# A fixed instruction order per engine in a pre-norm attention and GEGLU block, and another heir for two PSUM banks

## The chip, the core and the metric

One NeuronCore of a Trainium2 chip runs the whole program. Its engines are TensorE (PE in the profile; PEld is its loading of weights), VectorE (DVE), ScalarE (ACT), GpSimd (POOL) and SyncE (SP), which here issues nearly all DMAs. Each works through its own list of instructions in order, and waits on semaphores for the others. The metric is device microseconds per execution; several executions give a median.

## The reference, cut to what matters

x is 2048 rows of 512 floats. There are 32 heads of width 16 and four segments of 512 rows; attention is causal and inside a segment, and a running memory M, z joins the segments.

```python
h = x + A(layernorm(x))            # A: attention, then @ wo
out = h + B(layernorm(h))          # B: (gelu(y @ w_gate) * (y @ w_up)) @ w_down
# A, for segment s, heads in parallel:
p = softmax(qs @ ks.T / 4 + mask);  a_dot = p @ vs
a_mem = (phi(qs) @ M) / (phi(qs) @ z + 1e-6)       # phi(t) = t+1 if t>0 else exp(t)
o = g * a_mem + (1 - g) * a_dot                    # g = sigmoid(beta)
M += phi(ks).T @ vs;  z += sum(phi(ks))
```

The hidden width of B is 1376.

## The kernel before, in words

**Numbers.** Products are made in a reduced float type (fp32r) from operands split in two: a rounded copy on ScalarE (the "high" half) and the rest by a subtraction on VectorE or GpSimd. Three matmuls (SPLIT) make one product. So one entry of TensorE's order is often three 512-column matmuls.

**Attention.** Sixteen units U (four groups of eight heads, four segments) are cut into 32 halves Q of four heads each. For a unit, qkv projects (L634, the first time L646 for two at once) and moves the results by DMA into tiles stq and stk; vproj makes the values (L675); transposes (L754) and a small product (L762) renew the memory; mem reads it (L792 and L808 on TensorE, L810 on VectorE). For a half, two passes over the scores follow:

- pass_a, the row-maximum pass: scores into a bank of pool PA (L835), a masked maximum on VectorE (L843), small steps (L859, L862), a transpose (L866), and a DMA that puts the negated maximum as one more row into stq.
- pass_b, the other score pass: transposed scores, shifted by that row, into a bank of pool PB (L914, for the last diagonal block L906), the exponential on ScalarE (L922), masking on GpSimd (L925), and the product with the values in 32-column matmuls side by side in TensorE's four column groups (L946), into a bank of pool PPV. A half has eleven such score groups.

In the very last half, fill() in pass_b (L895) repeats a score matmul into a bank that pool PX holds at that time, up to ten times; nothing reads it.

**Seam and feed-forward.** wo_seg multiplies by wo per segment (operand split L1012 and L1014, matmuls L1019, sum L1023); ln2 normalises (L523, L575) and transposes (L594). The feed-forward runs twice over 1024 rows, in eleven hidden blocks f of 128 (the last 96); each block is seven products (prod, L1191; a Strassen-like scheme on two-by-two blocks), the gate (L1198 to L1222) and, for one or two blocks at a time, down (L1256, added up by L1264 and stored by L1269). Its weights are loaded into raw tiles (L1154), split (L1159 on ScalarE, L1161 on GpSimd) and combined (L1168 on GpSimd).

**PSUM.** Eight banks: three in PD, two in PA, two in PB, one in PPV. When nothing waits for a pool any more, its banks go to the pool named in `then`: PA's to PX, PB's and PPV's to PYZ (X, Y, Z are the banks of the feed-forward's products).

**What sets the order.** The code first registers 5308 groups of instructions with S.op, each with an engine, an assumed duration, a priority (formed from unit numbers and the table DUE) and the tiles that it reads, writes or takes. Nothing is issued by that. The group registered n-th has number n. Then Sched.run makes the order of all engines by list scheduling: among groups whose predecessors are placed and for which a buffer is free, it takes the earliest possible ones and among these the one with the lowest priority. It keeps a clock for each engine from the assumed durations; the clock also decides which of several free buffers a group gets. Where TensorE changes between normal matmuls (mode "f") and those in column groups (mode "c"), the clock adds DRAIN.

Each group is issued on its engine when it is placed, so the order in which run() places the groups of one engine is that engine's program.

## Time and profile before

| | us |
|---|---|
| median of 3 runs (823.0 to 824.62) | 824.03 |
| span of the profiled execution, first to last instruction | 820.5 |
| TensorE busy in it | 805.0 |
| VectorE busy | 615.2 |
| ScalarE busy | 561.7 |
| GpSimd busy | 483.8 |

The median is 3.5 us above the span, which begins with the first instruction and ends with the last. Busy time is the time in which at least one instruction of the engine runs; idle time in a row stands in brackets with the engine, tile and line that ended it. In tables of waits a row gives who waited, for whom, the sum in us, how often, and the longest. A weight load that waits stands for its matmul, which follows it in the same queue.

### The profile page before, as it was taken

Reading aid. Unit: us, or ns where it says so; the run is one execution under the profiler, and the core shown is the slowest. Engines: PE = TensorE matmul, PEld = TensorE weight load, DVE = VectorE, ACT = ScalarE, POOL = GpSimd, SP = SyncE. Lnnn points to the kernel's source line nnn. Section 1 sums busy time; section 2 is a strip of 40 time slices with the busy share of each in tenths; the row PEclk is TensorE's granted clock in tenths of the full one; section 3 lists DMA queues with packets and bytes.
Section 4 is the critical chain, followed back from the end, with each engine's and each line's share of the span. In section 5 each row is a group of like instructions: output and inputs, shape, how many; then the busy total and the mean of one; then the engine's idle time right before and its main releaser. Section 6 shows DMA issues by size and latency. Waiting matters only on the chain.

```text
span 820.5 us, 15349 instructions
## 1 busy us (share of the span) xinstructions
PE 805.0 (98%) x4728; PEld 629.1 (77%) x4728; DVE 615.2 (75%) x1823; ACT 561.7 (68%) x1131; POOL 483.8 (59%) x720
## 2 busy tenths in 40 slices
PE   7999999999999999999999999999999999999998
PEld 5786878777786877767666687878888887888886
DVE  7998778798898877799878764666657867565666
ACT  8689677899877868777676753786566454646450
POOL 8334334455344644456566884987797676869660
PEclk9999999999999999999999999999999999999999
DMA  7544445465564654466465763531211341212102
GB/s 243 143 115 131 133 126 135 131 199 157 139 176 115 185 157 122 124 172 186 140 188 165 234 205 125 165 93 52 65 39 52 108 152 38 78 40 64 52 1 102
DMA packets 71893, 103.51 MB, mean 126 GB/s; under 512 B 14340, under 2 KB 25156, under 8 KB 71812
## 3 DMA queue, kind: packets, MB, share of 16 engines
q1 hardware_dynamic: 71476, 102.15, 42.8%
q8 instruction: 37, 0.61, 0.3%
q10 hardware_dynamic: 336, 0.39, 0.2%
q14 instruction: 44, 0.36, 0.1%
HBM read 54.92 MB, written 21.43 MB: 93 GB/s over the span
## 4 chain that ended last, share of the span: by engine, by line
PE 88%; POOL 4%; DVE 4%; ACT 2%; issue 1%; DMA 1%; SPq 0%; POOLq 0%; ACTq 0%; DVEq 0%
PE bank L1191 23%; PE bank L1256 14%; PE bank L634 10%; PE bank L835 9%; PE bank L946 8%; PE bank L914 8%; PE bank L675 5%; PE bank L1019 5%; PE bank L762 1%; PE bank L808 1%; PE bank L594 1%; DVE bank L843 1%; PE bank L906 1%; POOL raw L1168 1%; DVE row L575 1%
## 5 line engine op out<-in xcount | busy, mean ns | idle before, releaser
L925 POOL TENSOR_SCALAR_AFFINE_SELECT pt<-pt 128x128 f32<-128x128 f32 (+2 forms) x352 | 119.4, 347 | 186.7 <-ACT pt L922 179.8
L922 ACT ACTIVATE pt<-bank 128x512 f32<-128x512 f32 (+1 forms) x352 | 182.2, 558 | 41.7 <-PE bank L914 32.2
L843 DVE CUSTOM_DVE_ANT_0 bank<-bank,amask 128x512 f32<-128x512 f32 (+1 forms) x256 | 157.0, 638 | 22.5 <-PE bank L835 20.7
L835 PE MATMUL bank<-stk,stq 128*128 128x512 f32 (+2 forms) x384 | 127.0, 374 | 0.6 <-DVE nm L843 0.2
L914 PE MATMUL bank<-stq,stk 128*128 128x384 f32 (+2 forms) x384 | 117.2, 359 | 2.1 <-ACT pt L922 2.0
L634 PE MATMUL bank<-xt,w 128*128 128x512 f32 x360 | 102.5, 396 | 0.1
L1264 DVE TENSOR_TENSOR pt<-pt,bank 128x512 f32<-128x512 f32 x95 | 64.4, 686 | 34.1 <-PE bank L1256 33.9
L843 DVE CUSTOM_DVE_ANT_0 aside<-bank,amask 128x256 f32<-128x256 f32 (+1 forms) x256 | 76.3, 353 | 14.2 <-PE bank L835 13.0
L914 PEld LDWEIGHTS bank<-stq,stk 128*128 128x128 f32 x384 | 68.0, 189 | 22.0 <-ACT pt L922 7.8
L835 PEld LDWEIGHTS bank<-stk,stq 128*128 128x128 f32 x384 | 68.7, 188 | 18.8 <-DVE nm L843 4.5
L946 PE MATMUL bank<-pt,vaug 128*32 128x512 f32 (+3 forms) x1024 | 76.9, 436 | 0.0
L634 PEld LDWEIGHTS bank<-xt,w 128*128 128x128 f32 x360 | 65.1, 188 | 10.5 <-DVE xt L604 0.4
L946 PEld LDWEIGHTS bank<-pt,vaug 128*32 128x32 f32 x1024 | 28.8, 109 | 40.2 <-issue 32.4
L843 DVE DVE_READ_ACCUMULATOR2_ANT nm<- 128x1 f32 x512 | 57.0, 111 | 0.0
L675 PE MATMUL bank<-wv,xt 128*128 128x256 f32 x384 | 55.6, 283 | 1.1 <-POOL wv L459 1.1
L675 PEld LDWEIGHTS bank<-wv,xt 128*128 128x128 f32 x384 | 52.4, 189 | 3.4 <-POOL wv L459 1.3
L443 POOL TENSOR_TENSOR w<-raw,w 128x512 fp32r<-128x512 f32 (+1 forms) x28 | 36.1, 1296 | 26.1 <-ACT w L438 25.9
L1161 POOL TENSOR_TENSOR w<-raw,w 128x512 fp32r<-128x512 f32 (+3 forms) x30 | 35.1, 1170 | 15.8 <-ACT w L1159 7.8
L1191 PE MATMUL bank<-xt,w 128*128 128x512 f32 (+1 forms) x159 | 43.5, 390 | 0.0
L1191 PE MATMUL bank<-xt,stk 128*128 128x512 f32 (+1 forms) x138 | 38.3, 391 | 0.0
L1161 POOL TENSOR_TENSOR stk<-raw,stk 128x512 fp32r<-128x512 f32 (+3 forms) x27 | 30.0, 1114 | 12.4 <-ACT stk L1159 12.3
L967 ACT ACTIVATE pvs<-bank 128x512 f32<-128x512 f32 x32 | 19.2, 599 | 26.1 <-PE bank L946 15.1
(305 smaller groups left out, 1873.6 us busy)
## 6 DMA issues: line engine op xcount, KB each, us to landing
stq<-hl SPq DMA_DIRECT2D x96, 128.0 KB
stk<-hl SPq DMA_DIRECT2D x188, 64.0 KB
pv_dram<-pvs SPq DMA_DIRECT2D x32, 256.0 KB
r<-r_dram SPq DMA_DIRECT2D x28, 256.0 KB
row<-x SPq DMA_DIRECT2D x24, 256.0 KB
raw<-wg SPq DMA_DIRECT2D x20, 256.0 KB
raw<-wu SPq DMA_DIRECT2D x20, 256.0 KB
raw<-wd SPq DMA_DIRECT2D x20, 256.0 KB
```

What stands on the lines that cost most here:

```text
L634: nc.tensor.matmul(pm.t, w.t[:, wi, dc * P:(dc + 1) * P], XT[s][dc].t[:, xi, :], start=dc == 0 and n == 0, stop=dc == ND - 1 and n == 2)
L675: nc.tensor.matmul(pm.t[:, 256 * t:256 * t + 256], XT[s][dc].t[:, xi, t0:t0 + P], whl[wi].t[:, h, 256 * (dc % 2):256 * (dc % 2) + 256], st ...
L835: nc.tensor.matmul(sa.t[:, k * w:(k + n) * w].rearrange("x (n w) -> x n w", n=n), sq.t[:, p, i * P:(i + 1) * P], sk.t[:, p, a:a + n, 0:w], ...
L843: nc.vector.tensor_tensor_reduce(out=(sa.t if i > 1 else aside)[:, k * w:(k + 1) * w], in0=sa.t[:, k * w:(k + 1) * w], in1=amask[:, D - w: ...
L914: nc.tensor.matmul(sc.t[:, lo:lo + D - q0], sk.t[:, p, a, q0:q0 + P], sq.t[:, p, q0:D], start=True, stop=True)
L922: act(w, prio, lambda: nc.scalar.activation(e.t[:, :w], sc.t[:, :w], AF.Exp), [sc], [e])
L925: nc.gpsimd.affine_select(v, v, pattern=pat + [[1, P]], compare_op=OP.is_ge, fill=0.0, base=0, channel_multiplier=-1)
L946: nc.tensor.matmul(pv.t[32 * n:32 * n + 32, kb * P:D], va.t[:, 136 * kb + 17 * j:136 * kb + 17 * j + 32], e.t[:, lo:lo + D - kb * P], star ...
L1161: pool(0.14 + 2.13e-3 * (hi - lo), prio, lambda: nc.gpsimd.tensor_tensor(v.t[:, 1, :hi - lo], r.t[:, lo:hi], v.t[:, 0, :hi - lo].bitcast(F ...
L1191: nc.tensor.matmul(dst.t[:w], v.t[:, wi, c0 + j * w:c0 + (j + 1) * w], b[bk][j].t[:, xi, :], start=first and j == 0 and n == 0, stop=j == ...
L1256: nc.tensor.matmul(pm.t[:, cs], HH[p, f, s][hi].t[:w, t * P:(t + 1) * P], v.t[:w, wi, cs], start=f == fl[0] and n == 0, stop=f == fl[-1] a ...
L1264: dve(W_, prio, lambda a=a, pm=pm, cs=cs, to=to: nc.vector.tensor_tensor(to.t[:, cs], a.t[:, cs], pm.t[:, cs], op=OP.add), [pm, a], [to])
```

## The change

It has four parts.

1. A list ORDER of 5308 numbers is added, and run() places the groups in this order, whatever their priority. The clock stays, for the choice of buffers; window, stay and DUE have no influence any more.
2. PA's two banks go to PB once nothing waits for PA, and PB's four go, once nothing waits for PB, one each to PX, PYZ, PX, PYZ. Before, PA's went straight to PX and PB's to PYZ.
3. The assumed durations of some TensorE groups (project, both score passes) rise by 0.004 to 0.012 us.
4. The code of the groups themselves is as before; every group of before is in the list once.

Groups that the text below speaks of by number: 43, 46 and 49 load the first wq, wk and wv (L437, L454); 930 to 932 load rows of the third segment (L614); 3303 and 3304 are the last memory product (L808) and its VectorE step (L810); 3494 is the last score group of the last half; 3593 and 3661 are the first transposes (L594) of the two norms at the seam, 3659 one of the last VectorE steps (L575) ahead of the latter; 3820 is the weights' rest (L443) of the third hidden block's down projection; 3857 and 3858 are the first split (L1159, L1161) of the fourth hidden block's weights and 4014 the first product (L1191) with them; 3758, 3759, 3768 and 3769 are operand splits of wo_seg (L1012, L1014).

```diff
+ORDER = [
+    6, 7, 5, 8, 2, 0, 4, 59, 13, 1, 3, 10, 930, 931, 932, 11, 9, 58, 30, 56, 57, 43, 46, 49, 12, 14, 15, 16, 17,
...
+    3476, 3477, 3660, 3482, 3483, 3303, 3479, 3480, 3382, 3658, 3487, 3491, 3659, 3494, 3485, 3486, 3821, 3304,
+    3488, 3489, 3661, 3667, 3535, 3536, 3700, 3492, 3493, 3824, 3495, 3496, 3458, 3662, 3663, 3713, 3701, 3668,
...
+    3745, 3756, 3750, 3957, 3715, 3958, 3751, 3960, 3857, 3820, 3856, 3752, 4626, 3962, 3858, 3757, 4627, 3753,
+    3758, 3766, 3963, 3964, 3754, 3961, 4014, 3859, 3759, 4017, 4015, 3860, 3767, 4016, 3869, 3760, 3755, 3965,
...
+]
...
-    def run(self, window=0.059, stay=0.1):
+    def run(self, order):
...
-        cand = [o for o in self.ops if o.n == 0]
-        order = []
+        done = []
...
-            first = min(e[0] for e in best)
-            _, at, o = min((e for e in best if e[0] <= first + window),
-                           key=lambda e: (e[2].prio, e[2].idx))
-            cand.remove(o)
...
+        for i in order:
+            o = self.ops[i]
+            assert o.n == 0, "an instruction comes before what it needs"
...
-    PA = Pool_(banks[3:5], then=PX)
-    PB = Pool_(banks[5:7], then=PYZ)
+    PB = Pool_(banks[5:7], then=Parts(1, PX, PYZ, PX, PYZ))
+    PA = Pool_(banks[3:5], then=PB)
...
-            pe(3 * mm(D), prio, f, [w, XT[s][dc]], [pm], acq=acq)
+            pe(3 * mm(D) + 0.012, prio, f, [w, XT[s][dc]], [pm], acq=acq)
...
-            m = mm(2 * w if i < 2 else w)
+            m = mm(2 * w if i < 2 else w) + 0.006
...
-                pe(2 * mm(2 * P), prio, f, [k3, q3], [sc], acq=[e], tail=mm(2 * P))
+                pe(2 * mm(2 * P) + 0.004, prio, f, [k3, q3], [sc], acq=[e], tail=mm(2 * P))
             else:
-                pe(len(parts) * mm(D - kb * P), prio, f, [sq, sk, mr], [sc], acq=[e],
+                pe(len(parts) * (mm(D - kb * P) + 0.005), prio, f, [sq, sk, mr], [sc], acq=[e],
                    tail=mm(D - kb * P))
...
-    return S.run()
+    return S.run(ORDER)
```

## The prediction

> **What bounds the kernel now.** I read the page first: how busy each engine is, then TensorE's and GpSimd's lines of the 40 slices.

> ```profile
> span 820.5 us, 15349 instructions
> PE 805.0 (98%) x4728; PEld 629.1 (77%) x4728; DVE 615.2 (75%) x1823; ACT 561.7 (68%) x1131; POOL 483.8 (59%) x720
> PE   7999999999999999999999999999999999999998
> POOL 8334334455344644456566884987797676869660
> ```

> TensorE (PE) has work in every slice, and no other engine comes near it. So a new order can only gain what TensorE loses between matmuls, and it leaves the count of real matmuls as it was. The chain of work that ended last gives TensorE's pace where nothing holds it: its start, its length, and how many matmuls follow each other.

> ```profile
> 597.02 11.61 PE bank L1191 x51
> 53.05 2.29 PE bank L946 x32
> 622.91 0.87 PE bank L594 x8
> 449.84 2.88 DVE row L575 x4
> ```

> A 512-column matmul takes 11.61 / 51 = 0.228 us, a product of the weights' 32 small matmuls (L946) 2.29, a transpose 0.87 / 8 = 0.109. The last row is of another kind: here the chain leaves TensorE for 2.9 us of VectorE. Where does that happen? The busy time by stretch (after the engines: DMA share and GB/s):

> ```profile
> 0.00:40.00 40.00, 33.68 (x187) 26.65 (x188) 32.38 (x104) 30.14 (x53) 23.10 (x48) 1.00 0.66 198
> 40.00:400.00 360.00, 358.50 (x2585) 274.40 (x2584) 301.80 (x1196) 289.16 (x615) 165.70 (x359) 1.00 0.52 147
> 400.00:460.00 60.00, 56.13 (x358) 37.92 (x360) 48.77 (x147) 44.69 (x91) 37.02 (x67) 1.00 0.56 164
> 460.00:560.00 100.00, 99.71 (x454) 78.93 (x447) 62.97 (x126) 63.68 (x130) 80.50 (x78) 1.00 0.51 159
> 560.00:640.00 80.00, 80.00 (x369) 66.18 (x368) 53.79 (x85) 50.18 (x91) 63.26 (x60) 1.00 0.20 54
> ```

> The columns are TensorE, its weight loads, VectorE (DVE), ScalarE (ACT), GpSimd (POOL). The idle time lies in the start (6.3 us) and at the seam between attention and feed-forward, 400 to 460 (3.9 us). From 560 on there is nothing to win. A busy matmul row hides short stalls, since a matmul is shown for 390 ns where the next follows after 228, so I also read the waits of the weight loads, which stand at the head of TensorE's queue. First 400 to 460, then 40 to 400 (total us, times, longest):

> ```profile
> PEld bank L914 <- ACT pt L922: 4.1, 8, 0.9
> PEld bank L594 <- DVE row L575: 2.6, 4, 1.3
> PEld bank L594 <- DVE z L800: 0.7, 1, 0.7
> ```

> ```profile
> PEld bank L946 <- issue: 27.5, 110, 0.4
> PEld bank L946 <- POOL pt L925: 4.7, 16, 0.4
> PEld bank L914 <- ACT pt L922: 3.6, 12, 0.8
> PEld bank L835 <- DVE nm L843: 2.2, 9, 0.4
> PEld bank L866 <- DVE mm L862: 1.5, 3, 0.7
> ```

> **The change, part by part.**

> *Ten filling matmuls.* fill() repeats a score matmul into a bank of PX, up to ten times, in the last group's score pass.

> ```profile
> L895 PE MATMUL bank<-stq,stk 128*128 128x512 f32 x10 | 3.9, 394 | 0.0
> 448.29 0.40 PE L895 MATMUL bank<-stq,stk 128*128 128x512 f32 x1
> 450.58 0.64 PE L594 MATMUL bank<-ident,row 128*128 128x128 f32 x2
> 452.30 1.22 PE L594 MATMUL bank<-ident,row 128*128 128x128 f32 x6 [1.08 <-DVE row L575]
> ```

> Now PX gets banks only through PB, which gives them up when its last score group (entry 3494) has taken its bank. So fill() finds a bank once at most: nine of ten go. At 0.228 that is 2.1 us, at most 2.3, at least nothing, if they only stood where TensorE would have waited. I take 2.0, since the score pass now has four banks at that place, not two.

> ```profile
> 4.49 4.05 PE L505 MATMUL bank<-ident 128*24 128x128 f32 x19
> ```

> At the kernel's start, after 4.3 us without a matmul, a transpose takes 4.05 / 19 = 0.213 us against 0.109 later: half the rate, though the granted clock stands at 1.00 in every stretch above. [...]

> *The score pass's banks.* In 400 to 460 eight score loads wait 4.1 us for ScalarE's exponentials to free one of two banks. A matmul in flight covers up to 0.228 of each, so 4.1 - 8 x 0.228 = 2.3 us is surely lost. The two further banks come only after the last row-maximum group, with 18 score groups to go in either order, which is about half of this stretch: 0 to 4.1, I take 1.5.

> *The second norm at the seam.* Old order: the first transposes (entry 3661) stand ten PE groups ahead of the last score group, and wait. The list puts them two places behind it; eight more score groups run first. It also puts VectorE's memory product (L810) behind the norm rather than ahead of it. For the first such norm (entry 3593) five score groups go ahead instead of three. Waits of 2.6 + 0.7: bounds 0 to 3.3, I take 2.0. Next late is then ScalarE: 44.7 of 60 us busy there, VectorE 48.8, so a stretch shortened by 5.5 us has VectorE at 48.8 / 54.5 = 90%. That is why I don't take it all.

> *The attention's steady part, 40 to 400.* The list is the old order with entries moved a few places: read by engine, an entry stands on average 5 places off on TensorE, 3 on ScalarE and VectorE, 2 on GpSimd, 4 on SP. Named waits add up to 4.7 + 3.6 + 2.2 + 1.5 = 12.0 us, 40 times; covered as above, 12.0 - 40 x 0.228 = 2.9 are surely lost. What decides is how much TensorE work lies between a group and the next but one, which takes its bank. Counted in groups at the pace above, the list has 23 score groups with under 1.2 us between (25 before) and 14 row-maximum groups (20 before). That is a slight relief: I take 2.0, between 12.0 gained (all of it) and 2.9 lost (as much again as is surely lost now), as each moved instruction also puts off those behind it on its engine. SP's queue is reordered too; no wait of TensorE in these tables names a load, so I count nothing for it, and a load that comes late belongs to the rival of new waits.

> *Excursions to the small matmuls.* The list enters the four-column mode 36 times, the old order 35. The wait ahead of L946 with nothing named costs 27.5 / 110 = 0.25 us: one more is 0.25 lost (0 to 0.4).

> *The start.*

> ```profile
> PE bank L505 <- DMA pt<-x: 4.3, 1, 4.3
> PE bank L675 <- POOL wv L459: 1.1, 1, 1.1
> 17.41 1.23 POOL wv L459
> ```

> Three row loads for the third norm (entries 930 to 932) now go ahead of the first weights on SP's queue, and ScalarE takes one of that norm's sums (L485) ahead of the first split and two of the copies that fill stk (L427) behind it. The first weights' rest on GpSimd comes later by a memset, but both L459 then follow each other with hardly anything between. The 1.1 us goes and the first product is late by about as much: I take 0.2 gained, from 1.1 gained to 2 lost.

> *Feed-forward.* Ordered anew too, with 0.3 us idle in 460 to 560 and none later: 0, from 0.3 gained; what could be lost is the slower rival. The edited costs and the new run() issue nothing; they only decide which free bank a group gets. The tail keeps its order, and its last store is issued behind the same two additions.

> **Sum:** 2.0 + 1.5 + 2.0 + 2.0 + 0.2 - 0.25 = 7.45, say 7.5 us. The profiled execution spans 820.5, the median is 824.0; the 3.5 between lie outside its first and last instruction and stay. Forecast: span 813.0, time **816.5 us**. Its own range is 812 to 820.5 (the steady part's term between 6.5 gained and 2 lost).

> **The rivals.**

> *The list closes most waits.* If the waits of both tables went (12.0 + 7.4 less the cover of 53 x 0.228 = 12.1, so 7.3 sure and 19.4 at most) beside the fills, the gain would be 9.3 to 21.4; what of it lies under the forecast's range is 803 to 812, about 808. For it: the span's own margin is larger than its 15.5 us of idle PE time. [...] Against: entries moved five places hardly reach 40 scattered waits.

> *New waits for the old.* VectorE at 301.8 of 360 us and ScalarE at 289.2 have little room, and a list made from fixed costs can't know when a DMA lands. Then only the fills stay and are eaten up: 822 to 826, about 824.

> *GpSimd is late for the fourth hidden block (slower).*

> ```profile
> 504.35 1.30 POOL L1014 TENSOR_TENSOR wv<-row,wv 128x512 fp32r<-128x512 f32 x1 [6.95 <-ACT wv L1012]
> 509.96 1.99 POOL L1161 TENSOR_TENSOR stk<-raw,stk 128x512 fp32r<-128x512 f32 x2 [4.32 <-ACT stk L1159]
> 509.25 0.63 ACT L1159 ACTIVATE stk<-raw 128x512 fp32r<-128x512 f32 x1 [4.99 <-DMA row<-o_dram]
> 512.47 0.85 PE L1191 MATMUL bank<-xt,stk 128*128 128x512 f32 x3
> ```

> The list puts this block's first product (entry 4014) 59 groups behind the last weights' product of the attention; it was 74. At 3 x 0.228 = 0.68 a group, TensorE comes there 10.2 us earlier. Its weights' split is moved up as well, ahead of the two L1014 for which GpSimd stood idle. But the split waited for ScalarE, and that for a buffer or a load. If this wait doesn't move up with it, TensorE stands still for those 10.2 us; behind the product are all other PE groups, and behind those the sums on VectorE. If the end of the wait stays where it is, the gains ahead of it (7) are lost as well: 824 + 10.2 less what stays of 0 to 7, so 827 to 834, about 830. It decides from the point where the split starts later than TensorE's arrival, 512.5 - 10.2 - 7, less its own 1.99 / 2: about 494. For it: GpSimd is at 80.5% there. Against: its idle 6.95 and 4.32 lie just there.

> *The hand-over does nothing.* ScalarE's exponentials set the seam, and four banks fill as two do: without the terms of fills and banks, 816.5 + 3.5 = 820.

> [...]

> **How the numbers follow.** Forecast (812 to 820.5) 0.50; most waits closed 0.15; new waits for old 0.16 (0.05 under 822.4, 0.09 within, 0.02 above 825.7); GpSimd late 0.13; the hand-over does nothing 0.04; clock gate 0.02. About 0.2% (1.6 us) is what a measurement of this kernel tells from no change. Faster: 0.50 + 0.15 + 0.05 + 0.04 + 0.02 = 0.76; same 0.09; slower 0.13 + 0.02 = 0.15. The range reaches to the middle of both outer rivals, **807 to 828**, and leaves out about 0.08 on each side.

> **What would show it.** L895 at most once; no wait of L594 for L575 over 0.5 us at the seam; L914's wait for L922 in 400 to 460 halved; the stretch before the last score group about 5 us shorter; waits in 40 to 400 down by 2. Wrong would be: a wait of L1191 for L1161 of some us between 485 and 515, or more waits of L835 for L843 than 9.

## The result and the profile after

The changed kernel takes **818.68 us** (median of 4 executions, 817.08 to 819.58) against 823.65 of the kernel before (4 executions, 823.0 to 824.62): ratio 0.9936, interval 0.9919 to 0.9954. A second measurement, among the last experiments, gave 820.3 us (12 executions) against 823.48 (35): ratio 0.9969, interval 0.9955 to 0.9982. So the change makes it faster by 0.3 to 0.6%, some 3 to 5 us. The forecast of 816.5 had the sign and too large a gain.

The profiled execution of after took 818.04 us and spans 816.3 us: 1.7 us lie outside the span, in this run as in nearly all that followed (1.7 or 1.8). So the profiled execution of before, with its span of 820.5, took about 822.2 us, less than any of the three times listed for it; the 3.5 us that the prediction laid outside the span were 1.7, and the rest was the difference from run to run.

The page of after, then the busy time by stretch, with the prediction's cuts:

```profile
span 816.3 us, 15144 instructions
PE 801.3 (98%) x4718; PEld 626.1 (77%) x4718; DVE 615.1 (75%) x1823; ACT 563.1 (69%) x1132; POOL 480.9 (59%) x720
```

```profile
0.00:40.00 40.00, 33.01 (x190) 26.84 (x191) 32.94 (x104) 30.03 (x53) 22.24 (x44) 1.00 0.65 194
40.00:400.00 360.00, 357.81 (x2573) 270.91 (x2573) 301.81 (x1184) 289.31 (x611) 160.70 (x356) 1.00 0.53 144
400.00:460.00 60.00, 58.21 (x389) 39.37 (x388) 49.63 (x157) 47.47 (x99) 42.04 (x75) 1.00 0.60 179
460.00:560.00 100.00, 99.56 (x438) 80.78 (x437) 61.83 (x118) 63.70 (x129) 79.64 (x77) 1.00 0.54 163
```

The ten fills are gone (4728 matmuls became 4718, and the line that was L895 has no row left). In 400 to 460 TensorE issues 389 matmuls where it issued 358, ten of those being fills. The ten microseconds in which it shows best stand here first for before, then for after:

```profile
450.00:460.00 10.00, 8.24 (x47) 5.26 (x49) 7.62 (x13) 8.09 (x17) 7.19 (x13) 1.00 0.51 160
```

```profile
450.00:460.00 10.00, 9.95 (x74) 6.86 (x74) 7.41 (x13) 8.82 (x20) 9.38 (x13) 1.00 0.57 171
```

The waits of the weight loads of after, first 40 to 400, then 400 to 460. A line of the helpers stands 274 lower than before: L1109 was L835, L1117 L843, L1188 L914, L1196 L922, L868 L594, L849 L575, L1220 L946, L1199 L925, L932 L658, L1028 L754, L1140 L866, L1136 L862.

```profile
PEld bank L1109 <- DVE nm L1117: 4.9, 13, 0.6
PEld bank L1220 <- POOL pt L1199: 4.8, 19, 0.4
PEld bank L1188 <- ACT pt L1196: 3.1, 12, 0.5
PEld bank L1028 <- DVE pk L932: 1.7, 3, 1.1
PEld bank L1140 <- DVE mm L1136: 0.3, 1, 0.3
```

```profile
PEld bank L1188 <- ACT pt L1196: 3.5, 9, 0.7
PEld bank L1109 <- DVE nm L1117: 1.6, 4, 0.5
PEld bank L868 <- DVE row L849: 1.1, 1, 1.1
```

At the seam the norm's wait fell from 2.6 to 1.1 us, and the one that is left lies ahead of 440. In the steady part the waits did not fall: L1109 waits thirteen times for VectorE's maximum, 4.9 us, where L835 waited nine times, 2.2. The four waits that the prediction added up to 12.0 are 4.8 + 3.1 + 4.9 + 0.3 = 13.1 here, L1028 waits 1.7 where L754 of before has no row, and all rows with a named cause add up to 22.0 us against 16.2.

**Where the time went**, stage by stage. From the trace, each matmul counts with the pace of its kind where nothing holds it: 0.227 us for 512 columns and in proportion for fewer, about twice as much in L946, L762, L792 and L808 (in before's trace a group of L946 takes 2.29 us, where its columns would make 1.14 at the other pace, eight matmuls of L762 with 136 columns take 0.93 where it would be 0.48, two of L808 with 512 take 0.86 where it would be 0.45, and four of L792 with 128, side by side, 0.11 where one would take 0.057), a quarter where four stand side by side, as those of L946 and L792 do, 0.109 for a transpose; fills don't count. The sum, 772 us, is the same for all kernels here, so one can read at which time each has reached the same work. Work 400 is reached by before at 435.1 us, 430 at 472.5; the seam's gain lies between them. The numbers are microseconds behind (+) or ahead of (-) the profiled execution of before:

```
work done                 200    300    400    430    500    772   seam (430 less 400)
before is there at      221.4  325.5  435.1  472.5  543.2  815.9
changed                  -0.9   +2.0   +1.6   -3.5   -3.9   -4.2   -5.1
changed, again           -0.3   +3.2   +4.2   -0.9   -1.0   -0.8   -5.1
old, then new            +0.6   +1.1   +0.6   -4.5   -4.6   -4.0   -5.1
new, then old            +0.1   +3.0   +3.2   +3.2   +2.8   +3.1    0.0
before without fills     +1.9   +1.5   +1.4   +1.2   +1.9   +2.6   -0.2
before, hand-over        +1.6   +1.1   +1.0   -2.1   -1.0   -0.1   -3.1
new list, two banks      -2.2   +1.6   +0.9   +2.5   +3.0   +2.9   +1.6
seam alone               +1.0   +1.2   +0.9   -4.2   +0.9   +0.6   -5.1
norm alone               +0.5   +0.1   +0.1   +2.2   +1.8   +1.3   +2.1
changed, with fills      -0.9   +2.4   +1.7   -1.9   -2.3   -2.7   -3.6
two banks, with fills    -1.3   +1.6   +0.9   +1.3   +2.3   +1.9   +0.4
hand-over, with fills    +3.2   +3.4   +3.3   +3.4   +3.5   +3.6   +0.1
three parts              -0.4   +3.0   +2.6   -2.5   -1.4   -1.5   -5.1
```

This can be read. The seam gains 5.1 us in every kernel that has its new order and the four banks (3.6 with fills put back), and in no other. Ahead of it, programs that are the same there differ from run to run (before without fills, with the hand-over, and with hand-over and fills lie 1.0 to 3.3 us behind before's own trace at work 400), so a time at one point says little. But these three are as far behind at work 200 already. From work 200 to 400 the six kernels with the old order there (before without fills, both with the hand-over, old then new, seam alone, norm alone) move by -0.6 to +0.1 us, and those with the new order there lose 2.2 to 3.1. The second trace of the changed kernel loses 4.5, but 1.6 of them by a half rate that comes up below. So the new order costs in this part, in every trace. At work 200 the kernels with the new start lie at -2.2 to +0.1 and the six others at +0.5 to +3.2: the new order is ahead there, by some 2 us on average.

Two lines hold a half rate (a granted clock of 0.50) between work 400 and 430 (see the runs): the new list with two banks 6.8 us of it, the hand-over with fills 3.4 us. If it costs half its length, an estimate, their seams would have gained up to 1.8 and 1.6 us without it.

### The profile page after: what moved, and what is told of

Read it like the earlier page. It is cut to its first block, busy times and chain, and to the rows that moved or that the text cites. A ratio compares the mean times of both kernels' runs of the same rounds, so it can differ in the third digit from the quotient of the medians.

```text
span 816.3 us, 15144 instructions
## 1 busy us (share of the span) xinstructions
PE 801.3 (98%) x4718; PEld 626.1 (77%) x4718; DVE 615.1 (75%) x1823; ACT 563.1 (69%) x1132; POOL 480.9 (59%) x720
## 4 chain that ended last, share of the span: by engine, by line
PE 83%; DVE 8%; ACT 3%; DMA 3%; issue 1%; POOL 1%; SPq 1%; ACTq 0%; DVEq 0%; POOLq 0%
PE bank L1465 24%; PE bank L1530 13%; PE bank L1109 8%; PE bank L908 8%; PE bank L1220 8%; PE bank L1188 7%; PE bank L1293 5%; PE bank L949 4%; DVE bank L1117 2%; PE bank L868 1%; PE bank L1082 1%; PE bank L1036 1%; DVE hl L991 1%; PE bank L1180 1%; DVE aside L1117 1%
## 5 line engine op out<-in xcount | busy, mean ns | idle before, releaser
L1199 POOL TENSOR_SCALAR_AFFINE_SELECT pt<-pt 128x128 f32<-128x128 f32 (+2 forms) x352 | 117.7, 348 | 186.7 <-ACT pt L1196 181.7
L1196 ACT ACTIVATE pt<-bank 128x512 f32<-128x512 f32 (+1 forms) x352 | 183.1, 558 | 49.3 <-PE bank L1188 41.8
L1117 DVE CUSTOM_DVE_ANT_0 bank<-bank,amask 128x512 f32<-128x512 f32 (+1 forms) x256 | 157.2, 638 | 25.2 <-PE bank L1109 22.5
L1109 PE MATMUL bank<-stk,stq 128*128 128x512 f32 (+2 forms) x384 | 131.8, 377 | 2.1 <-DVE nm L1117 0.8
L1188 PE MATMUL bank<-stq,stk 128*128 128x384 f32 (+2 forms) x384 | 114.6, 357 | 0.5 <-ACT pt L1196 0.4
L1117 DVE CUSTOM_DVE_ANT_0 aside<-bank,amask 128x256 f32<-128x256 f32 (+1 forms) x256 | 79.6, 353 | 17.7 <-PE bank L1109 13.8
L1109 PEld LDWEIGHTS bank<-stk,stq 128*128 128x128 f32 x384 | 69.9, 188 | 23.0 <-DVE nm L1117 6.9
L1188 PEld LDWEIGHTS bank<-stq,stk 128*128 128x128 f32 x384 | 67.5, 188 | 21.2 <-ACT pt L1196 6.6
L1220 PE MATMUL bank<-pt,vaug 128*32 128x512 f32 (+3 forms) x1024 | 77.6, 436 | 0.0
L1220 PEld LDWEIGHTS bank<-pt,vaug 128*32 128x32 f32 x1024 | 28.8, 109 | 40.7 <-issue 33.4
L1117 DVE DVE_READ_ACCUMULATOR2_ANT nm<- 128x1 f32 x512 | 56.7, 111 | 0.0
L1435 POOL TENSOR_TENSOR w<-raw,w 128x512 fp32r<-128x512 f32 (+3 forms) x37 | 41.9, 1133 | 21.5 <-ACT w L1433 21.4
L1465 PE MATMUL bank<-xt,w 128*128 128x512 f32 (+1 forms) x183 | 50.3, 390 | 0.0
L1465 PE MATMUL bank<-xt,stk 128*128 128x512 f32 (+1 forms) x153 | 41.9, 390 | 0.0
L1465 PE MATMUL bank<-stk,w 128*128 128x512 f32 (+1 forms) x147 | 41.4, 391 | 0.0
L1465 PEld LDWEIGHTS bank<-xt,w 128*128 128x128 f32 (+1 forms) x183 | 33.7, 185 | 7.5
L1472 ACT ACTIVATE vaug<-bank 128x512 f32<-128x512 f32 (+1 forms) x33 | 19.4, 592 | 24.5 <-PE bank L1465 24.4
```

Of the source, the lines that this page charges most:

```text
L1109: nc.tensor.matmul(sa.t[:, k * w:(k + n) * w].rearrange("x (n w) -> x n w", n=n), sq.t[:, p, i * P:(i + 1) * P], sk.t[:, p, a:a + n, 0:w], ...
L1117: nc.vector.tensor_tensor_reduce(out=(sa.t if i > 1 else aside)[:, k * w:(k + 1) * w], in0=sa.t[:, k * w:(k + 1) * w], in1=amask[:, D - w: ...
L1188: nc.tensor.matmul(sc.t[:, lo:lo + D - q0], sk.t[:, p, a, q0:q0 + P], sq.t[:, p, q0:D], start=True, stop=True)
L1196: act(w, prio, lambda: nc.scalar.activation(e.t[:, :w], sc.t[:, :w], AF.Exp), [sc], [e])
L1199: nc.gpsimd.affine_select(v, v, pattern=pat + [[1, P]], compare_op=OP.is_ge, fill=0.0, base=0, channel_multiplier=-1)
L1220: nc.tensor.matmul(pv.t[32 * n:32 * n + 32, kb * P:D], va.t[:, 136 * kb + 17 * j:136 * kb + 17 * j + 32], e.t[:, lo:lo + D - kb * P], star ...
```

## The experiments

Each was timed in several rounds beside the kernel before; the ratio is to that kernel on the same chip. Where a lower granted clock comes up, it is the mean over an execution as the runs list it.

**Fills alone.** Before, with no fill.

```diff
-            if Q == 31 and PX.free and len(fills) < 10:
+            if Q == 31 and PX.free and len(fills) < 0:
```

> The kernel before with fill() doing nothing: order, banks and costs unchanged, ten matmuls of L895 fewer. If the fills are plain work on TensorE's path, as the prediction's first term took them, 2.0 to 2.3 us less than before, about 821.5. If they only stand where TensorE waits for one of two banks anyway, 0 to 0.5 less, and the waits of L914 for L922 between 440 and 460 grow by about what the fills took.

Measured: 823.83 us, ratio 1.0008 (0.9998 to 1.0019). The 2.3 us of matmuls went and the time stayed. In its trace 450 to 460 holds 34 matmuls in place of 47, and the waits beside them grew (4.1 to 5.9, 2.6 to 3.0):

```profile
450.00:460.00 10.00, 7.13 (x34) 4.40 (x33) 7.62 (x12) 7.97 (x18) 7.46 (x13) 1.00 0.47 139
```

```profile
PEld bank L914 <- ACT pt L922: 5.9, 12, 1.2
PEld bank L594 <- DVE row L575: 3.0, 5, 1.3
```

The fills stood where TensorE would have waited. They do something else besides: the granted clock was 0.995 to 0.998 in 9 of these 11 executions, and 0.999 or 1.000 in all 29 of the kernel before beside them (and in all 99 of the three batches). What that is, the runs with two banks show. A price of it can't be seen here: the nine executions with the lower clock averaged 823.9 us, the other two 824.1.

**Banks alone.** Before, with list scheduling, and only the hand-over.

```diff
-    PA = Pool_(banks[3:5], then=PX)
-    PB = Pool_(banks[5:7], then=PYZ)
+    PB = Pool_(banks[5:7], then=Parts(1, PX, PYZ, PX, PYZ))
+    PA = Pool_(banks[3:5], then=PB)
```

> The kernel before with only the two pool lines changed (PA's banks go to PB); the old list scheduling makes the order. Theory that the seam's gain comes from the banks: 3 to 4 us less than before (ten fills to one, and half of the 4.1 us of score waits at the seam), about 820. Rival, the list's order makes the gain and the banks alone do little: 0 to 1 less, since the first transposes of the second norm still stand ahead of the last score groups and wait about 1 us.

Measured: 824.76 us, ratio 1.0020 (1.0007 to 1.0032): slower, which neither theory had. The seam gains 3.1 us in the profiled execution, and 2.0 are given back behind it, 1.4 of them in one wait for GpSimd's split:

```profile
PEld bank L914 <- ACT pt L922: 4.3, 9, 0.9
PEld bank L594 <- DVE row L575: 2.1, 5, 0.7
PEld bank L1191 <- POOL stk L1161: 1.4, 1, 1.4
```

With one fill left, 10 of 12 executions had a clock of 0.998 or less; the profiled one had 0.999 and 822.07 us.

**The old order as far as entry 3243, the new one behind it** (new pools, no fills). The list begins

```diff
-    6, 7, 5, 8, 2, 0, 4, 59, 13, 1, 3, 10, 930, 931, 932, 11, 9, 58, 30, 56, 57, 43, 46, 49, 12, 14, 15, 16, 17,
+    0, 5, 2, 1, 6, 7, 4, 3, 8, 43, 46, 30, 49, 55, 9, 108, 56, 109, 57, 13, 110, 10, 58, 59, 111, 11, 31, 61, 930, 12,
```

> The changed kernel with the old order, as a list, for the first 3243 groups (to about 400 us) and the new list's order behind. Theory that the seam gains some 4.5 us and that the new order of the steady part gives 2 back: faster than the changed kernel by 1 to 2 us, about 817. Rival, the new order helps in the steady part too as predicted (2.2 us with the start): slower than the changed kernel by 2, about 821.

Measured: 818.05 us, ratio 0.9942 (0.9929 to 0.9955). The whole gain lies behind entry 3243. This is level with the first measurement of the changed kernel (0.9936) and better than the second (0.9969), so the time decides between theory and rival no further.

**The new order as far as entry 3243, the old one behind it**, with the old pools and the fills; the edit is the reverse of the last.

> The new order for the first 3243 groups (to about 400 us), the old order behind, with the old pools, so with the fills and two score banks at the seam. Theory that the new order costs in the steady part: 1 to 2 us slower than before, about 825. The prediction's terms for start and steady part: 2.2 us faster than before, about 821.5.

Measured: 824.54 us, ratio 1.0021 (1.0008 to 1.0034). Start and steady part together cost about 1.7 us (0.7 to 2.8), where the prediction had 2.2 gained.

**Fills back in the changed kernel.**

```diff
-            if Q == 31 and PX.free and len(fills) < 10:
+            if Q == 31 and len(fills) < 10:
...
-                nc.tensor.matmul(PX.free[0][2], sk.t[:, 0, 0, 0:P], sq.t[:, 0], start=True, stop=True,
+                nc.tensor.matmul(sc.t, sk.t[:, 0, 0, 0:P], sq.t[:, 0], start=True, stop=True,
```

> The changed kernel with ten filling matmuls put back: in the last group's score pass each of the first ten score groups makes its first matmul twice into its own bank. Theory (the seam's new order gains because it puts TensorE's own work where it stood idle): nothing is left there to hide ten matmuls, so they cost up to 10 x 0.227 = 2.3 us and the gain against the kernel before falls from about 5 to 2.5 to 4 us. Rival (the seam is set by ScalarE's exponentials and VectorE in the new order too): the ten are hidden, gain 5 us as without them. In the old order taking them away was worth nothing (+0.7 us, within the noise).

Measured: 820.99 us, ratio 0.9972 (0.9959 to 0.9986), a gain of 2.3 us, a little under the theory's 2.5 to 4. At the seam 3.6 us are gained in place of 5.1: the ten matmuls, 2.3 us, cost 1.5 there. The time by itself does not settle it, since the changed kernel came out at 0.9936 and at 0.9969. The trace speaks for the theory: at the new seam most of a fill is no longer hidden.

**The new list with two banks.** Old pools, no fills, and four score groups five places later:

```diff
-    3378, 3462, 3463, 3466, 3469, 3472, 3455, 3456, 3460, 3624, 3464, 3465,
+    3378, 3462, 3463, 3466, 3455, 3456, 3460, 3624, 3464, 3469, 3465,
```

> The new list with the old pools (the row-maximum pass hands its banks back to both passes as before) and no filling matmul; four score groups at the seam (3469, 3472, 3484, 3494) stand five places later in the list because only then a bank is free. Theory (the order carries the gain, the banks alone gave nothing): 4 to 5 us faster than before, ratio 0.994 to 0.995. Rival (the list needs the four banks, with two of them the score groups that it pulls ahead wait for the exponentials): the waits of L1188 for L1196 between 440 and 465 come back and 2 to 4 us of the gain are lost, ratio 0.996 to 1.000. The prediction's own terms would have 1.5 us lost, 0.9955.

Measured: 823.16 us, ratio 1.0004 (0.9989 to 1.0020). The gain is gone; the theory that the order carries it without the banks fell. The waits (440 to 455) and then the clock (last but two of the columns) in its profiled execution:

```profile
PEld bank L1172 <- ACT pt L1180: 5.3, 9, 0.9
```

```profile
450.00:452.00 2.00, 1.63 (x4) 0.56 (x3) 1.82 (x8) 1.84 (x5) 1.04 (x4) 1.00 0.14 40
452.00:453.00 1.00, 0.44 (x1) 0.19 (x1) 1.00 (x3) 0.41 (x2) 0.41 (x1) 0.90 0.00 0
453.00:459.00 6.00, 5.54 (x16) 4.22 (x17) 0.81 (x2) 3.37 (x7) 2.17 (x5) 0.50 0.47 135
459.00:460.00 1.00, 1.00 (x7) 0.98 (x6) 0.07 (x1) 0.80 (x3) 1.00 (x3) 0.68 0.00 0
```

Nine score loads wait 5.3 us for the exponentials (L1172 and L1180 are before's L914 and L922). Behind that the granted clock is 0.50: 0.2 us of 452 to 453, the six after it and 0.64 of 459 to 460, together 6.84 us, which costs half of it, 3.4, by estimate. It then has only 16 matmuls in 6 us. Seven of its 12 executions had a clock of 0.996 to 0.998, on average 824.4 us; the five at 0.999 and 1.000 were at 821.8.

**The seam alone.** The changed kernel with the old order up to entry 3243, the new one for 480 entries, the old one behind.

> The changed kernel with the old order for the first 3243 entries, the new one for the next 480 (the seam, to about 476 us), and the old one for all of the feed-forward behind. Theory (the seam alone carries the gain): ratio 0.9945 to 0.996, 3.5 to 4.5 us faster than before. Rival (the feed-forward's new order is needed, since the old one has TensorE wait where the seam now delivers it earlier): a new stall of 1 to 4 us behind 476, ratio 0.996 to 1.000.

Measured: 822.59 us, ratio 0.9995 (0.9983 to 1.0008). The seam gains its 5.1 us and the next 20 give them back. The waits of 466 to 486 (L1449 are the feed-forward's products, L1277 those of wo_seg, L1456 the gate, L1270 and L1272 the operand splits):

```profile
PEld bank L1449 <- ACT pq L1456: 2.0, 1, 2.0
PEld bank L1277 <- POOL wv L1272: 1.8, 2, 1.1
PEld bank L1277 <- ACT wv L1270: 1.2, 1, 1.2
PEld bank L1449 <- ACT vaug L1456: 1.1, 1, 1.1
```

Before has 0.2 us of waits there, after none. TensorE comes five microseconds sooner and, in the old order, ScalarE and GpSimd do not.

**The second norm alone.** The old order as a list with the old pools and the fills; only 3303, 3304 and the four transposes, with the steps that hang on them, moved behind 3494.

```diff
-    3494, 3489, 3675, 3824,
+    3494, 3303, 3304, 3661, 3667, 3662, 3668, 3673, 3663, 3669, 3664, 3670, 3686,
```

> The old order given as a list, with the old pools and the ten filling matmuls; moved are only the second norm's four transposes at the seam and the memory product (3303, 3304), from up to ten groups ahead of the last score group to right behind it, as the new list has them. The prediction's term says 2.0 us (0 to 3.3): ratio 0.9975. Theory (the gain needs work that has no wait in front of it, and the score groups now standing ahead still wait for their banks): L594's wait for L575 goes, L914's for L922 grows, 0 to 1 us faster, ratio 0.999 to 1.001.

Measured: 824.26 us, ratio 1.0015 (1.0004 to 1.0026): slower, which neither figure had. Up to work 400 this list follows before's trace within 0.1 us at the points 300 and 400, so it is a fair copy of the old order. The wait for the norm did not shorten the seam; it became two others, and the stretch is 2.1 us longer (440 to 470; L852 is L594, L1306 one of VectorE's later steps for wo_seg's operand):

```profile
PEld bank L1172 <- ACT pt L1180: 2.3, 6, 0.7
PEld bank L852 <- DVE vaug L1306: 1.8, 1, 1.8
```

**Two banks with fills.** The new list with two banks, and ten fills put in as in the changed kernel with fills.

> The new list with the old pools, as in the run with two banks, plus ten filling matmuls (each of the last group's first ten score groups makes its first matmul twice into its own bank). In the run with two banks and no fills the granted clock stood at 0.50 from about 452.8 to 459.5 us, after a run of waits for the exponentials. Theory (the fills keep the clock up where the banks run short, and what the four banks are worth is mostly the half rate that they make impossible): the granted clock stays at 0.999 or 1.000 in all its runs, the ten matmuls hide in the waits, and the time falls from 823.2 to 820 to 822, ratio 0.996 to 0.9985. Rival (the waits for the exponentials themselves are the price, and the half rate a by-product): the time stays at 822.5 to 824, ratio 0.9995 to 1.001, with the clock at 1.000.

Measured: 824.9 us, ratio 1.0027 (1.0015 to 1.0039): slower, and outside what either theory gave. The clock was at 0.999 or 1.000 in 9 of 12 executions instead of 5 of 12, so the fills do keep it up more often; but at a full clock the time is 825.0 (9 executions) against 821.8 without them (5), beside 823.3 and 823.0 of before in their batches. The waits for the exponentials stay (fills are L1151, scores L1170), and the fills now wait themselves, with the score groups behind them:

```profile
PEld bank L1151 <- ACT pt L1177: 2.9, 5, 1.0
PEld bank L1170 <- ACT pt L1177: 2.4, 4, 0.8
```

So the half rate is not the whole price of two banks. At a full clock the list with two banks gains 1.2 us (821.8 against 823.0), the changed kernel in its second measurement 3.4 (820.0 against 823.3): some 2 us go to the waits, and the half rate takes the rest.

**Banks alone, fills kept.** Before with the hand-over and ten fills.

> The kernel before, list scheduling, with only the hand-over of the banks and with ten filling matmuls kept (in the score groups' own banks): the banks alone, without the loss of the fills. With the hand-over and one fill the time was 824.8 and the granted clock 0.995 to 0.999. Theory (the loss there was the half rate, and the banks alone gain about what the prediction gave them): clock 0.999 to 1.000, ratio 0.997 to 0.9995, 0.5 to 2.5 us faster than before. Rival (the banks alone give nothing because the next wait takes over, L1191 for GpSimd's split at 488): ratio 1.000 to 1.002, whatever the clock.

Measured: 823.96 us, ratio 1.0010 (0.9996 to 1.0023): the rival's figure, but with another cause. Nine executions at a full clock average 823.0, against 823.3 of before there, so the banks alone gain nothing even then. In the profile the score groups come sooner and the norm's transposes wait as long as before (longest 1.3 us there too):

```profile
PEld bank L594 <- DVE row L575: 2.3, 4, 1.3
```

Behind that wait the clock stood at 0.50 here too, for 3.4 us between 457 and 461.

**Three parts.** The changed kernel with the old order between its first 1770 entries and entry 3243.

> The changed kernel with a list made of three: its own first 1770 entries (to about 221 us), the old order from there to the first 3243 entries, and its own behind. In the trace of the changed kernel the new order was about 0.9 us ahead of the old by 221 us and lost 2.9 us between 221 and 326, on waits for VectorE. Theory (these differences belong to the order): 1 to 2 us faster than the changed kernel, 816 to 817.5, ratio 0.992 to 0.9932. Rival (they are the jitter of a single execution, as the list of the old start with the new rest came out level with the changed kernel): 818 to 819, ratio 0.9935 to 0.995.

Measured: 820.89 us, ratio 0.9971 (0.9957 to 0.9986): level with the changed kernel beside it, as the rival had it, though both are slower than its 818 to 819. The trace says something else. The run loses 3.4 us from work 200 to 300, nearly all of them in a few microseconds behind the joint of the two lists, at 221 us, where transposes wait for ScalarE and VectorE as in neither of the kernels that were joined:

```profile
222.66 0.66 PE L852 MATMUL bank<-ident,row 128*128 128x128 f32 x4 [1.30 <-ACT vaug L944]
223.87 0.66 PE L852 MATMUL bank<-ident,row 128*128 128x128 f32 x4 [0.56 <-DVE xt L862]
```

Behind these the old order loses nothing: from work 210 to 370 the run moves from +2.8 to +3.0, the changed kernel from -0.5 to +2.0. So the old order does cure the loss there, and the joint cost as much; the time alone could not tell this from jitter.

**The changed kernel again**, unedited.

> The changed kernel itself, on the same chip as the three others, for a direct comparison: all theories expect a ratio of 0.992 to 0.9954 to the kernel before, 818 to 819 us, and the granted clock at 0.999 to 1.000.

Measured: 820.3 us, ratio 0.9969 (0.9955 to 0.9982); clock 0.997 or 0.998 in 5 of 12 executions, 821.5 us on average, and 820.0 in the other seven. No theory expected that. The profiled execution has a clock of 0.998 and shows the cause. First its waits of 425 to 432, which are those of the first trace to the tenth; then the clock:

```profile
PEld bank L1188 <- ACT pt L1196: 0.9, 2, 0.7
PEld bank L1109 <- DVE nm L1117: 0.9, 2, 0.5
PEld bank L1140 <- DVE mm L1136: 0.3, 1, 0.3
```

```profile
430.00:431.00 1.00, 0.87 (x4) 0.67 (x4) 0.96 (x5) 0.00 (x0) 1.00 (x1) 0.93 0.76 223
431.00:432.00 1.00, 1.00 (x4) 0.90 (x3) 1.00 (x4) 0.02 (x1) 0.37 (x2) 0.50 0.03 10
432.00:433.00 1.00, 1.00 (x3) 0.74 (x3) 0.47 (x2) 0.47 (x1) 0.00 (x0) 0.50 0.11 16
433.00:434.00 1.00, 1.00 (x5) 0.88 (x4) 0.00 (x0) 0.31 (x1) 0.00 (x0) 0.50 0.61 223
434.00:435.00 1.00, 1.00 (x7) 0.83 (x5) 0.04 (x1) 0.70 (x2) 0.65 (x2) 0.86 0.76 125
```

```profile
433.45 1.24 PE L1293 MATMUL bank<-w,wv 128*128 128x512 f32 x3
```

The same three matmuls in the first trace of this kernel:

```profile
431.25 0.86 PE L1293 MATMUL bank<-w,wv 128*128 128x512 f32 x3
```

0.14 us of 430 to 431, three whole microseconds and 0.28 of the last stand at half rate: 3.42 us, half of the 6.84 in the run with two banks. Half of 3.42 is 1.7 us, the estimate of the loss; the traces show 1.6: ahead of it the same matmuls start 1.0 us behind the first trace (L1293 at 426.02 and 425.02), after it 2.6 (L1188 at 435.63 and 433.05). The averages above differ by 1.5.

## Why the prediction was right or wrong

**What bounds the kernel: right.** All that was won lies where TensorE loses between matmuls, and most of it in 400 to 460.

**Fills (2.0): right only together with the rest.** Alone they were worth nothing, the lower bound that was named ("if they only stood where TensorE would have waited"). At the new seam they would cost 1.5 of their 2.3 us. The prediction chose 2.0 because of the four banks, and that reason held.

**Banks (1.5) and norm (2.0): not terms of a sum.** Alone, banks gave 0.4 us at most (at a full clock, fills kept) and the norm's move -1.2 us: a wait that is taken away is taken over by the next, VectorE's row for the banks, the exponentials and L1306 for the norm. With the rest in place the banks are worth nearly all of the gain: without them the ratio is 1.0004, and 1.2 us are left at a full clock. For the three terms together the prediction had 5.5 us, and the seam gained 5.1. That sum was right; its parts were not additive. Of "what would show it", L895 and the stretch by 5 us came true; L914's wait in 400 to 460 went from 4.1 only to 3.5, not to half; and the wait for L575 that is left, 1.1, is over the 0.5 that was named.

**Steady part (2.0): the step that failed.** Waits of 40 to 400 were to fall by 2. The four named ones rose from 12.0 to 13.1, all named ones from 16.2 to 22.0, and from work 200 to 400 every trace with the new order lost 2.2 us or more. The step's reason was fewer score groups close behind the one whose bank they take (23 for 25) and fewer such row-maximum groups (14 for 20). But L1109's wait for VectorE's maximum rose from nine times to thirteen, which the prediction itself had named as a sign of being wrong. The count looked at TensorE's work between two groups and not at when VectorE comes to the maximum; that this is the reason is argued, no run changes it alone.

**Start (0.2): too small.** At work 200 the new order is some 2 us ahead on average. With the loss behind, start and steady part together cost 1.7 us (0.7 to 2.8) in the run made for them, where 2.2 gained were forecast.

**Feed-forward (0): right, for a reason that was missed.** The new order wins nothing there, but it is needed to keep the seam's gain: with the old one 4.8 of the 5.1 us are lost again. The rival that had GpSimd late for L1191 was of this kind. It did not strike the changed kernel, whose list moves the splits as well; it struck kernels that gave TensorE its gain without that: the hand-over (L1191 for L1161, 1.4 us) and, with other waits for ScalarE and GpSimd, the seam alone.

**The half rate: given 0.02, and it came.** The "clock gate" among the chances is a half rate at the seam once the fills are gone. In the second trace of the changed kernel the granted clock stands at 0.50 for 3.42 us, behind five waits of at most 0.7 us within 4 us, and this costs 1.6 us; a clock of 0.997 or 0.998 stands in 5 of this kernel's 16 executions. In two other traces it comes behind short waits too: of at most 0.9 us with two banks (0.50 for 6.84 us), of at most 1.3 us in the hand-over with fills (3.4 us). The longest wait does not tell whether it comes: before's trace has one of 1.3 us in 400 to 460 and a clock of 1.00 there, and the first trace of the changed kernel has the waits of the second to the tenth and a clock of 1.00. What decides is not shown.

How often it comes differs from kernel to kernel. With the pools and the fill() of before (before, norm alone, new then old) 1 of 123 executions had a clock under 0.999, of the ten other kernels 49 of 117: before without its fills 9 of 11, the changed kernel 5 of 16. Of the slow transposes at the start (0.213 us each) the granted clock tells nothing: in before's trace it has its first record at 8.2 us, and they lie at 4.5 to 8.5, so the 1.00 shown for 0 to 40 doesn't speak of them.

**The base.** 816.5 was the span of 813.0 plus 3.5. With 1.7, the same sum would have said 814.7, against 818.0 for the profiled execution: its gain was 4.2 us, against 7.5. So the 3.5 hid 1.8 us of what the steady part's term was off by: that the forecast came within 2.2 us of 818.68 is to that extent luck.

Shown are: the seam's 5.1 us, that they need the order, the banks and the feed-forward's order together, that the fills were hidden in before, and that they kept its clock up (under 0.999 in 9 of 11 executions without them, in none of 99 with them). Not shown is that this saved before any time, nor which wait of the steady part costs how much.

No version was better than the change. The one with the old start and steady part (0.9942) is level with it.

## What to carry to other kernels

Terms for stalls that lie one behind the other on a path cannot be added up: undo each part alone, and both "it is worth nothing" and "it is worth all" can come out. When one engine is to arrive sooner, move the work of the engines that feed it up with it, past the end of the stretch, or the gain is returned there. And before a matmul that nothing reads is struck out, look at the granted clock of many executions, not only at the wait beside it: before without its fills hardly changed in time (823.83 us, ratio 1.0008), but its clock was under 0.999 in 9 of 11 executions.
